# Top-k attention and a low-rank mixer: division by row sums moved to the side of the features, a pair's loads dealt out over four steps

## The chip, the cores and the metric

The kernel runs on one core of a Trainium2 chip. The metric is device time in microseconds; lower is better. All data are 32-bit floats.

## The reference

Attention over 8 batches, 8 heads, 576 positions and 64 features keeps for each query the 32 largest scores, and its output goes through a mixer: a low-rank mix over positions, then a two-layer network over the 512 channels.

```python
scores = scale * np.matmul(q, k.transpose(0, 1, 3, 2))
kth = np.partition(scores, -32, axis=-1)[..., -32:-31]
scores = np.where(scores >= kth, scores, -1e9)
attn = np.exp(scores - np.max(scores, axis=-1, keepdims=True))
attn = attn / (np.sum(attn, axis=-1, keepdims=True) + 1e-09)
x = heads_side_by_side(np.matmul(attn, v))      # (8, 576, 512)
h = x.transpose(0, 2, 1) @ U @ V                # U: 576x32, V: 32x576
u = x + h.transpose(0, 2, 1)
out = u + np.maximum(u @ w_ch1, 0.0) @ w_ch2    # 512 -> 2048 -> 512
```

## The kernel before

Two heads of one batch make a pair, so there are 32 pairs, four to a batch. The 576 positions are four tiles of 128 (t = 0 to 3) and an end of 64, called NT = 4, in which the two heads' ends lie one above the other in the 128 rows.

The order of the work is written out by hand: nothing is reordered by a planner. The main loop runs over steps. In the first four pairs (20 steps, up to ALONE) each tile has its own step; from pair 4 on (NPAIR) a pair has four steps, and the fourth takes tile 3 and the end together. In step n several tiles are in flight:

- `scores` (L332, L364) and `fold` of the tile after this one: PE's products, ACT's copies (L377), POOL's fold of each row's two halves (L428) and, after DVE's maximum (L430), its second half (L431);
- `front`: DVE's search for the 32 largest (L481 to L516), then ACT's and POOL's masking (L542 to L546) and ACT's exponentials, which sum each row into `den` (L435, L556);
- `blocks` turns the exponentials by 32x32 blocks on DVE (L572) and writes them to DRAM (`away`, issued by SP); `back` reads them as PT one step later (issued by ACT, L587);
- `values` of the tile three steps back: PE multiplies PT by V (L646, L649), with the features on the rows of the result, and ACT copies it to XT (L658). For the end (t = NT) positions are on the rows instead (L633), and ACT multiplies by the inverse sums into X (L641);
- `mixed`, once per pair: PE turns XT so that positions lie on the rows (L672), ACT copies it to X (L676), POOL multiplies by the inverse sums (L677). A step later PE multiplies by U (L688), ACT copies that to Tb (L696), PE multiplies by V (L700) and adds X turned back again in the same PSUM tile (L702), and ACT copies the sum to uT (L710), features on the rows.

The two-layer network of a batch (`mlp`: L742 with relu on ACT at L755, L760, turned back for the output at L784) is cut into single matmuls and dealt out by `fill`, eight times a step. Each fill adds a share to an account and issues matmuls until the account is used up:

```python
MLP_WORK = 2 * NF * NC * S / C
SLOTS, LONG, EARLY = 8, 1.4, 0.91
share = MLP_WORK / (NPAIR * SLOTS * (NT - 1 + LONG))
```

A fill also moves `mixed` on by one `yield`. After the last step the rest of the sixth batch's network runs, and then the last batch's, written out as `closing` with seven half-size products in place of eight (L836).

Loads are issued by SP. For pairs after the fifth q and k come in blocks of 32 features, eight DMAs each (L255, L260), and DVE turns them in one instruction (L302); v takes five DMAs (L284 to L288). `loading(g + 1)` issues q in step t = 0 of pair g, and k and v in step t = 1; the turning at L302 stands at the end of step t = 2.

Of the kernel before, what the change touches and what calls it, by code (L numbers as in the profile page):

```python
# [8 lines left out]
F32 = mybir.dt.float32  # L9
# [3 lines left out]
ALU = mybir.AluOpType  # L13
# [13 lines left out]
def kernel(  # L27
# [28 lines left out]
    nc = tc.nc  # L56
    B, H, S, D = q.shape
    P = 128
# [4 lines left out]
    NT, TAIL = 4, 64  # L63
    MAIN = NT * P
    HALF = S // 2
    assert S == MAIN + TAIL and D == 64 and H % 2 == 0 and C == 512 and TOPK % 8 == 0
    NPAIR = H // 2
    NP = B * NPAIR

    CH = NT + 1  # L70
    ALONE = NPAIR * CH
# [4 lines left out]
    BLK = 32  # L76
# [4 lines left out]
    const = ctx.enter_context(tc.tile_pool(name="const", bufs=1))  # L81
# [16 lines left out]
    ident = const.tile([P, P], F32, name="ident")  # L98
# [5 lines left out]
    vds = [const.tile([P, P], F32, name=f"vd{i}") for i in range(NV)]  # L104
    vts = [const.tile([P, 2, D], F32, name=f"vt{i}") for i in range(NV)]

    xs = [const.tile([P, NT + 1, P], F32, name=f"x{i}") for i in range(2)]
    for i in range(NV):
        nc.gpsimd.memset(vds[i], 0.0)
        nc.gpsimd.memset(vts[i], 0.0)  # L110
    for x in xs:
        nc.gpsimd.memset(x[:, NT, :], 0.0)
    W1Q = F // NT
    w1s = [const.tile([P, NC, W1Q], F32, name=f"w1{i}") for i in range(NT)]
    w2 = const.tile([P, NF, C], F32, name="w2")
    U = const.tile([P, NT + 1, R], F32, name="U")

    V = const.tile([NT * R, S], F32, name="V")
    four = const.tile([P, 1], F32, name="four")
    nc.vector.memset(four, -4.0)  # L120

# [8 lines left out]
    def cols(t):  # L130
        return slice(t * P, t * P + rows(t))

    def at(t):
        return slice(OFF[t], OFF[t] + rows(t))

    def half(h):
        return slice(h * D, (h + 1) * D)
# [96 lines left out]

    raw, qkTs, S2s, uTs, XTs, dens = {}, {}, {}, {}, {}, {}
    probs, PTs, folds, fronts_of = {}, {}, {}, {}
    inverted, aways = set(), {}

    def load(g):

# [2 lines left out]
    def loading(g):  # L243

        b, h0 = g // NPAIR, 2 * (g % NPAIR)
        ld = loads.tile([P, 2 * S], F32, tag="ld", name="ld")
        if blocked(g):
            for i, src in enumerate((q, k)):
                if i:
                    yield  # L250
                for a in range(4):
                    ds = src[b, h0 + a // 2, :, a % 2 * BLK : (a % 2 + 1) * BLK]
                    to = ld[a * BLK : (a + 1) * BLK, i * S : (i + 1) * S]
                    lead = TAIL if i and a >= 2 else 0
                    nc.sync.dma_start(  # L255
                        to[:, lead : lead + MAIN].rearrange("i (t m d) -> i t m d", t=NT, d=BLK),
                        ds[0:MAIN].rearrange("(m i t) d -> i t m d", i=BLK, t=NT),
                    )
                    end = 0 if lead else MAIN
                    nc.sync.dma_start(  # L260
                        to[:, end : end + TAIL].rearrange("i (m d) -> i m d", d=BLK),
                        ds[MAIN:S].rearrange("(m i) d -> i m d", i=BLK),
                    )
            raw[g] = ld
        else:
            tiles = []
            ends = ld[:, 2 * MAIN : 2 * S].rearrange("p (h d) -> p h d", h=2)
            for j, src in enumerate((q, k)):
                t = ld[:, j * MAIN : (j + 1) * MAIN].rearrange("p (t h d) -> p t h d", t=NT, h=2)
                for i in range(2):  # L270
                    queue = nc.scalar if g == 0 and i else nc.sync
                    queue.dma_start(
                        t[:, :, i, :],
                        src[b, h0 + i, 0:MAIN, :].rearrange("(p t) d -> p t d", t=NT),
                    )
                tiles.append(t)
            for i, src in enumerate((q, k)):
                nc.sync.dma_start(
                    ends[half(i)], src[b, h0 : h0 + 2, MAIN:S, :].rearrange("h p d -> p h d")
                )  # L280
            raw[g] = tiles, ends
        va, vd, vt = (a[g % NV] for a in (vas, vds, vts))
        for i in range(2):
            nc.sync.dma_start(  # L284
                va[:, i], v[b, h0 + i, 0:MAIN, :].rearrange("(p t) d -> p t d", t=NT)
            )
            nc.sync.dma_start(vd[half(i), half(i)], v[b, h0 + i, MAIN:S, :])
        nc.sync.dma_start(vt[TAIL:P], v[b, h0 : h0 + 2, MAIN:S, :].rearrange("h p d -> p h d"))  # L288
        yield
# [327 lines left out]
    def inverse(g, lo, hi):  # L617
        den = dens[g][:, lo:hi]
        if g == NPAIR - 1:
            nc.vector.tensor_scalar_add(den, den, 1e-9)  # L620
        nc.vector.reciprocal(den, den)

    def values(g, t):

        PT = PTs.pop((g, t))
        va, vd, vt = (a[g % NV] for a in (vas, vds, vts))
        O = ps_t.tile([P, P], F32, tag="tp", name="O")
        if t == NT:
            den, x = dens[g], xs[g % 2]
            if g not in inverted:  # L630
                inverse(g, 2 * NT if g == NPAIR - 1 else 0, 2 * NT + 1)
            for j in range(NT + 1):
                nc.tensor.matmul(  # L633
                    O,
                    lhsT=PT[:, j],
                    rhs=va[:, :, j, :] if j < NT else vt,
                    start=(j == 0),
                    stop=(j == NT),
                )
            for h in range(2):  # L640
                nc.scalar.mul(x[half(h), NT, half(h)], O[half(h), half(h)], den[half(h), 2 * NT :])  # L641
            return
        if shared(g, t):
            PT = PT.rearrange("p c n -> p (c n)")
            PT = PT.rearrange("p (a c j) -> p c a j", a=4, j=BLK)
        nc.tensor.matmul(O, lhsT=vd, rhs=PT[:, 2 * NT], start=True, stop=False)  # L646
        for j in range(NT):
            for h in range(2):
                nc.tensor.matmul(  # L649
                    O[half(h)],  # L650
                    lhsT=va[:, h, j, :],
                    rhs=PT[:, NT * h + j],
                    start=False,
                    stop=(j == NT - 1),
                )
        if t == 0:
            XTs[g] = attn.tile([P, MAIN], F32, tag="XT", name="XT", bufs=1)
        nc.scalar.copy(XTs[g][:, cols(t)], O)  # L658


    def mixed(g, wait, lag=0):
# [4 lines left out]
        if gi == 0:  # L666
            uTs[b] = mlpp.tile([P, NC, S], F32, tag="uT", name="uT")
        XT, den = XTs.pop(g), dens[g]
        X = xs[g % 2]
        tp = ps_t.tile([P, NT, P], F32, tag="tp", name="tp")  # L670
        for t in range(NT):
            nc.tensor.transpose(tp[:, t, :], XT[:, cols(t)], ident)  # L672
        X4 = X[:, 0:NT, :].rearrange("p t (h d) -> p t h d", h=2)
        tp4 = tp.rearrange("p t (h d) -> p t h d", h=2)
        den4 = den[:, 0 : 2 * NT].rearrange("p (t h) -> p t h ()", h=2).to_broadcast([P, NT, 2, D])
        nc.scalar.copy(X4, tp4)  # L676
        nc.gpsimd.tensor_tensor(X4, X4, den4, ALU.mult)  # L677
        if wait is None:
            waiting.append(g)
            while g in waiting:  # L680
# [5 lines left out]
        for t in range(NT + 1):  # L686
# [5 lines left out]
                start=(t < NT),  # L692
                stop=(0 < t),
            )
        Tb = mlpp.tile([P, P], F32, tag="Tb", name="Tb")
        nc.scalar.copy(Tb, pT)  # L696
        yield
        for chunks, (lo, hi) in zip(PARTS, SPAN):
            up = ps_t.tile([P, WIDE], F32, tag="tp", name="up")
            nc.tensor.matmul(up[:, 0 : hi - lo], lhsT=Tb, rhs=V[:, lo:hi], start=True, stop=False)  # L700
            for t in chunks:
                nc.tensor.matmul(  # L702
                    up[:, OFF[t] - lo : OFF[t] - lo + rows(t)],
                    lhsT=X[:, t, :],
                    rhs=ident if t < NT else ident2,
                    is_transpose=True if t < NT else None,
                    start=False,
                    stop=(t == chunks[-1]),
                )
            nc.scalar.copy(uTs[b][:, gi, lo:hi], up[:, 0 : hi - lo])  # L710
            yield
        if gi == NPAIR - 1:
            fillers.append(closing(b) if b == B - 1 else mlp(b))
# [371 lines left out]
    def tiles(n):  # L1085

        return steps[n] if 0 <= n < STEPS else []

    def weighted(m):

        for g, t in reversed(tiles(m)):
            values(g, t)
        if tiles(m)[-1][1] == NT:
            mixing.append(mixed(g, None, 1) if m < STEPS - 1 else mixed(g, 5, 0))
# [19 lines left out]
    for n in range(STEPS + 2):  # L1114
# [11 lines left out]
        if n >= ALONE - 1 and n <= ALONE:  # L1126
# [33 lines left out]
            next(here)  # L1160
            coming = loading(g + 1)
            next(coming)
            next(here)
            fill()
            continue
# [48 lines left out]
        turn()  # L1214
        fill()
        next(last, None)
        next(here, None)
        next_params(1)
        fill()
        if n >= STEPS:  # L1220
            weighted(n - 2)
        elif n - 2 >= ALONE and len(tiles(n - 2)) > 1:
            g2 = steps[n - 2][0][0]
            inverted.add(g2)
            inverse(g2, 0, 2 * NT + 1)
        next(here, None)
        bound = tiles(n + 1)[:1] == [(NPAIR + 1, 0)]
        if not bound:
# [8 lines left out]
            if shared(*tile_):  # L1237
                blocks(*tile_)
        turning = turned(n - 1)
        if n < STEPS and t < 2 and g + 1 < NP:  # L1240
            if t == 0:
                coming = loading(g + 1)
            next(coming)
        next(ready, None)
        if t != 0:
            next_params(1)
# [38 lines left out]
```

## Time and profile before

| what | value |
|---|---|
| median of 3 runs | 1685.39 us (1684.06 to 1687.28) |
| profiled execution: time, span | 1686.28 us, 1684.5 us |
| PE, weight loads, DVE busy | 94%, 72%, 92% of the span |
| ACT, POOL busy | 59%, 56% |
| mean granted clock | 0.969 |
| DMA | 273898 packets, 180.97 MB, 107 GB/s mean |

PE is TensorE's matmul, PEld its weight load, DVE VectorE, ACT ScalarE, POOL GpSimd, SP SyncE; a "q" after a name means its sequencer, which issues DMAs. A 32-bit matmul appears as two records. In a line of a group, "x20 | 14.6, 728" is 20 instructions, 14.6 us of busy time and 728 ns each; what follows is the idle time ahead of them and what ended it. L numbers are lines of the kernel before.

### The profile page before, as it was taken

Reading aid. Unit: us, or ns where it says so; the run is one execution under the profiler, and the core shown is the slowest. Engines: PE = TensorE matmul, PEld = TensorE weight load, DVE = VectorE, ACT = ScalarE, POOL = GpSimd, SP = SyncE. Lnnn points to the kernel's source line nnn. Section 1 sums busy time; section 2 is a strip of 40 time slices with the busy share of each in tenths; the row PEclk is TensorE's granted clock in tenths of the full one; section 3 lists DMA queues with packets and bytes.
Section 4 is the critical chain, followed back from the end, with each engine's and each line's share of the span. In section 5 each row is a group of like instructions: output and inputs, shape, how many; then the busy total and the mean of one; then the engine's idle time right before and its main releaser. Section 6 shows DMA issues by size and latency. Waiting matters only on the chain.

```text
span 1684.5 us, 29512 instructions
## 1 busy us (share of the span) xinstructions
PE 1586.0 (94%) x9498; PEld 1213.4 (72%) x9498; DVE 1543.7 (92%) x4364; ACT 1000.1 (59%) x2475; POOL 939.0 (56%) x741
## 2 busy tenths in 40 slices
PE   4666799999899999999999999999999999999999
PEld 2444466788677887788777887778777887778876
DVE  7999998999999999999999999999999999994452
ACT  4888778665665656565665656565665656554320
POOL 4778668655555555555555555555555455552620
PEclk7788799999999999999999999999999999999999
DMA  3323232254545555554545555554545455533001
GB/s 87 96 75 96 58 91 73 55 133 123 131 110 136 125 131 128 131 129 120 128 117 130 125 130 125 132 125 125 128 115 131 122 134 124 131 105 102 10 1 29
DMA packets 273898, 180.97 MB, mean 107 GB/s; under 512 B 171376, under 2 KB 258256, under 8 KB 273744
## 3 DMA queue, kind: packets, MB, share of 16 engines
q1 hardware_dynamic: 257712, 117.49, 30.2%
q10 hardware_dynamic: 16032, 61.61, 11.7%
q8 instruction: 75, 1.23, 0.3%
q14 instruction: 79, 0.65, 0.1%
HBM read 108.23 MB, written 70.78 MB: 106 GB/s over the span
## 4 chain that ended last, share of the span: by engine, by line
PE 54%; DVE 32%; SPq 4%; DMA 4%; issue 2%; POOL 2%; ACT 1%; DVEq 0%; ACTq 0%; POOLq 0%
PE mm L760 16%; PE mm L742 16%; DVE m L516 10%; DVE upper L511 9%; PE sc L332 4%; PE O L649 4%; DVE first L498 3%; PE mm L836 3%; DVE y L572 3%; DVE upper L483 2%; PE sc L836 2%; PE tp L836 2%; DVE place L511 2%; DMA ld<-in_k_dram 2%; SPq L255 2%
## 5 line engine op out<-in xcount | busy, mean ns | idle before, releaser
L742 PE MATMUL mm<-uT,w 128*128 128x320 f32 (+1 forms) x1792 | 461.1, 410 | 1.9 <-ACT hT L755 1.9
L760 PE MATMUL mm<-hT,w 128*128 128x320 f32 (+1 forms) x1792 | 461.5, 408 | 0.0
L546 POOL TENSOR_TENSOR Ssb<-Ssb,E 128x576 f32<-128x576 f32 x243 | 339.4, 1416 | 210.7 <-ACT E L545 210.4
L742 PEld LDWEIGHTS mm<-uT,w 128*128 128x128 f32 x1792 | 333.7, 191 | 97.5 <-issue 12.0
L760 PEld LDWEIGHTS mm<-hT,w 128*128 128x128 f32 x1792 | 330.5, 190 | 90.3 <-issue 10.2
L516 DVE MAX8 m<-upper 128x8 f32<-128x304 f32 (+1 forms) x780 | 367.4, 512 | 0.7
L511 DVE MATCH_REPLACE8 upper<-m,upper 128x304 f32<-128x304 f32 (+1 forms) x520 | 259.9, 507 | 0.0
L431 POOL TENSOR_TENSOR lower<-lower,upper 128x576 uint32<-128x576 uint32 x108 | 152.3, 1410 | 157.5 <-DVE upper L430 152.6
L428 POOL TENSOR_TENSOR lower<-Ssb 128x576 uint32<-128x576 uint32 x108 | 152.4, 1411 | 144.0 <-ACT Ssb L377 87.0
L435 ACT ACTIVATE Ssb<-Ssb,nmax 128x576 f32<-128x576 f32 x258 | 200.8, 780 | 22.3 <-POOL Ssb L522 10.1
L332 PE MATMUL sc<-qkT 64*128 64x288 f32 (+1 forms) x1056 | 178.8, 460 | 10.8 <-ACT Ssb L386 7.8
L545 ACT ACTIVATE E<-Ssb,least 128x576 f32<-128x576 f32 x243 | 176.2, 768 | 4.2
L483 DVE MAX8 upper<-lower 128x8 f32<-128x288 f32 x432 | 172.2, 440 | 6.9 <-POOL lower L431 6.9
L377 ACT COPY Ssb<-sc 128x576 f32<-128x576 f32 x216 | 127.6, 643 | 69.2 <-PE sc L332 69.1
L572 DVE STREAM_TRANSPOSE y<-Ssb 128x512 f32<-128x512 f32 (+1 forms) x312 | 155.4, 547 | 8.8 <-ACT Ssb L435 8.8
L755 ACT ACTIVATE hT<-mm 128x320 f32<-128x320 f32 (+1 forms) x224 | 92.1, 411 | 112.2 <-PE mm L742 107.4
L649 PE MATMUL O<-PT,va 128*64 128x128 f32 x2048 | 145.1, 286 | 0.0
L332 PEld LDWEIGHTS sc<-qkT 64*128 64x128 f32 (+1 forms) x1056 | 95.7, 197 | 51.2 <-issue 16.4
L649 PEld LDWEIGHTS O<-PT,va 128*64 128x64 f32 x2048 | 113.8, 141 | 16.3 <-issue 1.6
L511 DVE MATCH_REPLACE8 upper<-first,upper 128x304 f32<-128x304 f32 x216 | 97.7, 460 | 0.0
L481 DVE MATCH_REPLACE8 lower<-upper,lower 128x288 f32<-128x288 f32 x216 | 94.1, 444 | 0.0
L430 DVE TENSOR_TENSOR upper<-sc,Ssb 128x576 f32<-128x576 f32 x108 | 80.3, 744 | 12.7 <-ACT Stail L397 12.4
(250 smaller groups left out, 2201.3 us busy)
## 6 DMA issues: line engine op xcount, KB each, us to landing
away<-y SPq DMA_DIRECT2D x416, 144.0 KB, 2.5
PT<-away ACTq DMA_DIRECT2D x104, 576.0 KB, 3.9
raw<-in_moe_w_ch_dram SPq DMA_DIRECT2D x32, 512.0 KB, 3.8
va<-in_v_dram SPq DMA_DIRECT2D x64, 128.0 KB, 2.6
out_dram<-ob SPq DMA_DIRECT2D x59, 128.0 KB, 2.5
ld<-in_q_dram SPq DMA_DIRECT2D x108, 64.0 KB, 3.1
ld<-in_k_dram SPq DMA_DIRECT2D x108, 64.0 KB, 2.6
ld<-in_q_dram SPq DMA_DIRECT2D x108, 8.0 KB, 3.2
```

Of the source, the lines that this page charges most:

```text
L332: nc.tensor.matmul(out, lhsT=qkT[half(h), 0, cols(t)], rhs=qkT[half(h), 1, lo:hi], start=True, stop=True,)
L428: nc.gpsimd.tensor_tensor(bottom, a.bitcast(U32), b.bitcast(U32), ALU.add)
L435: nc.scalar.activation(E, chunk, AF.Exp, bias=nmax, scale=SCALE, accum_out=total)
L483: nc.vector.max(spot, lower)
L511: nc.vector.match_replace(nxt, ms[c], curs[c], NEG)
L516: nc.vector.max(ms[c], curs[c])
L545: nc.scalar.activation(gap, chunk, AF.Relu, bias=least[:, c : c + 1], scale=-WIDEN)
L546: nc.gpsimd.tensor_tensor(chunk, chunk, gap, ALU.subtract)
L572: nc.vector.transpose(y[:, :, i * NT : i * NT + c].rearrange("p r c j -> p c r j"), E2[:, a : a + c * P].rearrange("p (c r j) -> p c r j", ...
L649: nc.tensor.matmul(O[half(h)], lhsT=va[:, h, j, :], rhs=PT[:, NT * h + j], start=False, stop=(j == NT - 1),)
L742: nc.tensor.matmul(ph[:, 0:w], lhsT=first_layer(cc, f), rhs=uT[:, cc, lo:hi], start=(cc == 0), stop=(cc == NC - 1),)
L760: nc.tensor.matmul(po[:, 0:w], lhsT=w2[:, f, c * P : (c + 1) * P], rhs=hTs[f][:, 0:w], start=(f == 0), stop=(f == NF - 1),)
```

## The change

For the 28 pairs from NPAIR on, the division moves. The inverse sums are turned on DVE, written to DRAM in rows (four DMAs from SP), and read back as a tile `sc` that has features on the rows and the inverse sum of each position along them (four DMAs from ACT, broadcast over 64 rows each). POOL multiplies XT by it into uT. PE turns uT (and its end) for the product with U only; L702 is left out, and POOL adds the product with V to uT instead. The end's values are computed with features on the rows, 64 columns at a time. X and Tb have one buffer instead of two. Values of a step run in the order tile 3, end. The loads of a pair start one step sooner and are dealt out: q, half of k, half of k, v.

```diff
@@ -104,18 +104,19 @@
...
-    xs = [const.tile([P, NT + 1, P], F32, name=f"x{i}") for i in range(2)]
+    X = const.tile([P, NT + 1, P], F32, name="x")
...
+    upright = const.tile([P, BLK], F32, name="upright")
+    nc.vector.memset(upright, 0.0)
...
@@ -249,6 +250,8 @@
                 if i:
                     yield
                 for a in range(4):
+                    if i and a == 2:
+                        yield
                     ds = src[b, h0 + a // 2, :, a % 2 * BLK : (a % 2 + 1) * BLK]
                     to = ld[a * BLK : (a + 1) * BLK, i * S : (i + 1) * S]
                     lead = TAIL if i and a >= 2 else 0
@@ -262,6 +265,7 @@
                         ds[MAIN:S].rearrange("(m i) d -> i m d", i=BLK),
                     )
             raw[g] = ld
+            yield
         else:
             tiles = []
             ends = ld[:, 2 * MAIN : 2 * S].rearrange("p (h d) -> p h d", h=2)
@@ -618,7 +622,33 @@
         den = dens[g][:, lo:hi]
         if g == NPAIR - 1:
             nc.vector.tensor_scalar_add(den, den, 1e-9)
-        nc.vector.reciprocal(den, den)
+        if g < NPAIR:
+            nc.vector.reciprocal(den, den)
+            return
+        inverted.add(g)
+        nc.vector.reciprocal(upright[:, 0 : 2 * NT + 1], den)
+        turned_ = small.tile([P, BLK], F32, tag="rows", name="rows", bufs=1)
+        nc.vector.transpose(turned_, upright)
+        rd = dram.tile([2 * NT + 1, P], F32, tag="rd", name="rd")
+        scales[g] = rd
+        for a in range(4):
+            nc.sync.dma_start(
+                rd[:, a * BLK : (a + 1) * BLK], turned_[a * BLK : a * BLK + 2 * NT + 1]
+            )
+
+    def scale(g):
+
+        rd = scales.pop(g)
+        sc = attn.tile([P, S], F32, tag="scale", name="scale", bufs=1)
+        scales[g] = sc
+        for h in range(2):
+            nc.scalar.dma_start(
+                sc[half(h), 0:MAIN].rearrange("p (t n) -> p t n", t=NT),
+                rd[0 : 2 * NT].rearrange("(t h) n -> h t n", h=2)[h : h + 1].to_broadcast([D, NT, P]),
+            )
+            nc.scalar.dma_start(
+                sc[half(h), MAIN:S], rd[2 * NT : 2 * NT + 1, half(h)].to_broadcast([D, TAIL])
+            )
 
     def values(g, t):
 
@@ -626,7 +656,19 @@
         va, vd, vt = (a[g % NV] for a in (vas, vds, vts))
         O = ps_t.tile([P, P], F32, tag="tp", name="O")
         if t == NT:
-            den, x = dens[g], xs[g % 2]
+            if g >= NPAIR:
+                for j in range(NT + 1):
+                    for h in range(2):
+                        nc.tensor.matmul(
+                            O[half(h), 0:TAIL],
+                            lhsT=va[:, h, j, :] if j < NT else vt[:, h, :],
+                            rhs=PT[:, j, half(h)],
+                            start=(j == 0),
+                            stop=(j == NT),
+                        )
+                nc.scalar.copy(XTs[g][:, MAIN:S], O[:, 0:TAIL])
+                return
+            den = dens[g]
             if g not in inverted:
                 inverse(g, 2 * NT if g == NPAIR - 1 else 0, 2 * NT + 1)
             for j in range(NT + 1):
@@ -638,7 +680,7 @@
                     stop=(j == NT),
                 )
             for h in range(2):
-                nc.scalar.mul(x[half(h), NT, half(h)], O[half(h), half(h)], den[half(h), 2 * NT :])
+                nc.scalar.mul(X[half(h), NT, half(h)], O[half(h), half(h)], den[half(h), 2 * NT :])
             return
         if shared(g, t):
             PT = PT.rearrange("p c n -> p (c n)")
@@ -654,7 +696,7 @@
                     stop=(j == NT - 1),
                 )
         if t == 0:
-            XTs[g] = attn.tile([P, MAIN], F32, tag="XT", name="XT", bufs=1)
+            XTs[g] = attn.tile([P, S], F32, tag="XT", name="XT", bufs=1)
         nc.scalar.copy(XTs[g][:, cols(t)], O)
 
 
@@ -666,15 +708,35 @@
         if gi == 0:
             uTs[b] = mlpp.tile([P, NC, S], F32, tag="uT", name="uT")
         XT, den = XTs.pop(g), dens[g]
-        X = xs[g % 2]
+        uT = uTs[b][:, gi]
+        if g >= NPAIR:
+            sc = scales.pop(g)
+            pairs_ = [
+                a[:, 0:MAIN].rearrange("p (b n) -> p b n", b=2) for a in (XT, sc)
+            ]
+            ends = [uT[:, OFF[t] : OFF[t] + 2 * P] for t in (0, 2)]
+            for i, end in enumerate(ends):
+                nc.gpsimd.tensor_tensor(end, pairs_[0][:, i], pairs_[1][:, i], ALU.mult)
+            nc.gpsimd.tensor_tensor(uT[:, at(NT)], XT[:, MAIN:S], sc[:, MAIN:S], ALU.mult)
+            yield
+            yield
         tp = ps_t.tile([P, NT, P], F32, tag="tp", name="tp")
         for t in range(NT):
-            nc.tensor.transpose(tp[:, t, :], XT[:, cols(t)], ident)
-        X4 = X[:, 0:NT, :].rearrange("p t (h d) -> p t h d", h=2)
-        tp4 = tp.rearrange("p t (h d) -> p t h d", h=2)
-        den4 = den[:, 0 : 2 * NT].rearrange("p (t h) -> p t h ()", h=2).to_broadcast([P, NT, 2, D])
-        nc.scalar.copy(X4, tp4)
-        nc.gpsimd.tensor_tensor(X4, X4, den4, ALU.mult)
+            nc.tensor.transpose(
+                tp[:, t, :], XT[:, cols(t)] if g < NPAIR else uT[:, at(t)], ident
+            )
+        X4 = X[:, 0:NT, :]
+        nc.scalar.copy(X4, tp)
+        if g < NPAIR:
+            X4 = X4.rearrange("p t (h d) -> p t h d", h=2)
+            den4 = den[:, 0 : 2 * NT].rearrange("p (t h) -> p t h ()", h=2)
+            nc.gpsimd.tensor_tensor(X4, X4, den4.to_broadcast([P, NT, 2, D]), ALU.mult)
+        else:
+            if g == NPAIR:
+                nc.gpsimd.memset(X[TAIL:P, NT, :], 0.0)
+            tp = ps_t.tile([P, P], F32, tag="tp", name="tp")
+            nc.tensor.transpose(tp[0:TAIL], uT[:, at(NT)], ident)
+            nc.scalar.copy(X[0:TAIL, NT, :], tp[0:TAIL])
         if wait is None:
             waiting.append(g)
             while g in waiting:
@@ -692,13 +754,15 @@
                 start=(t < NT),
                 stop=(0 < t),
             )
-        Tb = mlpp.tile([P, P], F32, tag="Tb", name="Tb")
+        Tb = mlpp.tile([P, P], F32, tag="Tb", name="Tb", bufs=1)
         nc.scalar.copy(Tb, pT)
         yield
         for chunks, (lo, hi) in zip(PARTS, SPAN):
             up = ps_t.tile([P, WIDE], F32, tag="tp", name="up")
-            nc.tensor.matmul(up[:, 0 : hi - lo], lhsT=Tb, rhs=V[:, lo:hi], start=True, stop=False)
-            for t in chunks:
+            nc.tensor.matmul(
+                up[:, 0 : hi - lo], lhsT=Tb, rhs=V[:, lo:hi], start=True, stop=(g >= NPAIR)
+            )
+            for t in chunks if g < NPAIR else ():
                 nc.tensor.matmul(
                     up[:, OFF[t] - lo : OFF[t] - lo + rows(t)],
                     lhsT=X[:, t, :],
@@ -707,7 +771,11 @@
                     start=False,
                     stop=(t == chunks[-1]),
                 )
-            nc.scalar.copy(uTs[b][:, gi, lo:hi], up[:, 0 : hi - lo])
+            if g < NPAIR:
+                nc.scalar.copy(uT[:, lo:hi], up[:, 0 : hi - lo])
+            else:
+                nc.scalar.copy(sc[:, lo:hi], up[:, 0 : hi - lo])
+                nc.gpsimd.tensor_tensor(uT[:, lo:hi], uT[:, lo:hi], sc[:, lo:hi], ALU.add)
             yield
         if gi == NPAIR - 1:
             fillers.append(closing(b) if b == B - 1 else mlp(b))
@@ -1088,7 +1156,7 @@
 
     def weighted(m):
 
-        for g, t in reversed(tiles(m)):
+        for g, t in tiles(m):
             values(g, t)
         if tiles(m)[-1][1] == NT:
             mixing.append(mixed(g, None, 1) if m < STEPS - 1 else mixed(g, 5, 0))
@@ -1159,6 +1227,7 @@
             split(*steps[n + 1][0])
             next(here)
             coming = loading(g + 1)
+            next(coming)
             next(coming)
             next(here)
             fill()
@@ -1214,15 +1283,16 @@
         turn()
         fill()
         next(last, None)
+        if n < STEPS and n - 2 >= ALONE and len(tiles(n - 2)) > 1:
+            scale(steps[n - 2][0][0])
         next(here, None)
         next_params(1)
         fill()
         if n >= STEPS:
+            if n == STEPS:
+                inverse(NP - 1, 0, 2 * NT + 1)
+                scale(NP - 1)
             weighted(n - 2)
-        elif n - 2 >= ALONE and len(tiles(n - 2)) > 1:
-            g2 = steps[n - 2][0][0]
-            inverted.add(g2)
-            inverse(g2, 0, 2 * NT + 1)
         next(here, None)
         bound = tiles(n + 1)[:1] == [(NPAIR + 1, 0)]
         if not bound:
@@ -1237,10 +1307,12 @@
             if shared(*tile_):
                 blocks(*tile_)
         turning = turned(n - 1)
-        if n < STEPS and t < 2 and g + 1 < NP:
-            if t == 0:
-                coming = loading(g + 1)
-            next(coming)
+        if n < STEPS and n - 1 >= ALONE and len(tiles(n - 1)) > 1:
+            inverse(steps[n - 1][0][0], 0, 2 * NT + 1)
+        if n < STEPS:
+            if t == NT - 1:
+                coming = loading(g + 2) if g + 2 < NP else iter(())
+            next(coming, None)
         next(ready, None)
         if t != 0:
             next_params(1)
```

More of the change, by code (lines that the diff above doesn't have):

```diff
@@ L110 @@
         nc.gpsimd.memset(vts[i], 0.0)
-    for x in xs:
-        nc.gpsimd.memset(x[:, NT, :], 0.0)
+    nc.gpsimd.memset(X[:, NT, :], 0.0)
     W1Q = F // NT
@@ L236 @@
     probs, PTs, folds, fronts_of = {}, {}, {}, {}
-    inverted, aways = set(), {}
+    inverted, aways, scales = set(), {}, {}
     def load(g):
```

## The prediction

> **What bounds the kernel now.** I read the page first: PE is busy for 94% of the span and DVE for 92%, so the shares alone don't decide. Next I read the table of windows over the steady part, in 50 us stretches (columns: wall time, then PE, weight load, DVE, ACT and POOL busy, granted clock, DMA share, GB/s):
>
> ```profile
> 850.00:900.00 50.00, 50.00 (x289) 36.17 (x288) 49.52 (x150) 29.56 (x74) 29.10 (x23) 1.00 0.51 130
> 900.00:950.00 50.00, 50.00 (x312) 39.91 (x311) 47.92 (x143) 29.65 (x77) 26.73 (x21) 1.00 0.50 124
> ```
>
> PE fills its stretches, DVE leaves about 1 us per pair of heads free. Then the chain of waits from 840 to 960 us, which is PE from end to end. Here is one step and the start of the next (start, length, what, records):
>
> ```profile
> 890.43 1.11 PE O L633 x10
> 891.55 0.22 PE O L646 x2
> 891.77 1.02 PE O L649 x16
> 892.79 1.18 PE sc L364 x14
> 893.97 1.17 PE sc L332 x8
> 895.14 1.27 PE mm L760 x4
> 896.42 0.44 PE tp L672 x4
> 896.85 4.85 PE mm L760 x18
> ...
> 906.62 0.74 PE up L700 x2
> 907.35 0.39 PE up L702 x4
> 907.74 1.13 PE mm L760 x4
> 908.87 0.43 PE up L700 x2
> 909.31 0.22 PE up L702 x2
> ```
>
> Each piece starts where the one before ends: PE is back to back, and a 320-column record takes 4.85/18 = 0.27 us, which is its full rate. From about 448 to 1493 us no PE record starts late by more than its usual spacing, over 22 pairs of 47.4 us. So a saving on PE counts in full there, a new PE wait counts in full, and a DVE wait counts for nothing until PE has given up about 1 us per pair. Before 448 us (pairs 4 to 6) DVE is full and the pair takes 46.4 us; after 1493 us PE works off what is left and then closes.
>
> **What the Trainium skill says.** "TensorEngine Tiling (Array Packing)", section Key Properties: column tiles run their weight loads and matmuls in parallel, and a change of tiling mode drains the array. The trace agrees: 16 records of L649 (64 columns, 128 moving) take 1.02 us, 0.064 each, where a 128-column record of L633 takes 0.11. "GPSIMD Engine Reference", section 3.1 Elementwise, has POOL at about twice DVE's time for an add; the trace shows POOL's own times, used below. "DMA: Bandwidth & Descriptors", Rules for kernel authors, wants the issuing engine to wait on the semaphore of a DMA whose bytes it reads back through another DMA. No wait of that length is on PE's chain before; the new inverse sums need one, on ACT.
>
> **The change part by part, per changed pair** (28 of them, 22 in the PE-bound stretch).
>
> *PE, removed.* The second turning of X, L702: 0.39 + 0.22 = 0.61 us. *PE, added:* one turning of the 64-row end, priced as one of the four of L672: 0.44/4 = 0.11. *PE, changed:* the tail's values, L633, 10 records of 128x128 in 1.11 us, become 20 records of 64 columns by 64 moving, in the tiling mode of L649. Upper bound: L649's 0.064 each, 1.28 us, that is 0.17 more than now. Lower bound: each moves half the columns, and L649's 1.02 contains a change of mode that the tail right behind it doesn't pay again (estimated 0.15 us): (1.02 - 0.15)/16/2 x 20 = 0.54. I take 0.56, because L649 shows its records running side by side: saved 0.55. Sum on PE: -0.61 + 0.11 - 0.55 = **-1.05 us** (ends -0.33 and -1.07).
>
> *PE, a new wait.* Before, L672 turns XT as soon as ACT has copied it, and PE waits for nobody. Now POOL first multiplies XT by the scales into uT, and PE turns uT two fills later. Is two fills enough? In the order of the code the multiplications stand behind this step's fold on POOL. The timeline gives that queue:
>
> ```profile
> 896.02 1.42 POOL L428 TENSOR_TENSOR lower<-Ssb 128x576 uint32<-128x576 uint32 x1 [1.90 <-issue]
> 897.93 1.04 POOL L677 TENSOR_TENSOR x<-x,den 128x512 f32<-128x512 f32 x1 [0.50 <-ACT x L676]
> 898.93 1.40 POOL L431 TENSOR_TENSOR lower<-lower,upper 128x576 uint32<-128x576 uint32 x1
> ```
>
> L428 ends at 897.44, 2.3 us after the scores end at 895.14, and it hangs on those scores through ACT's copies, so it can't come earlier relative to PE. POOL's price for 128x256 is this group:
>
> ```profile
> L772 POOL TENSOR_TENSOR oT<-oT,uT 128x256 f32<-128x256 f32 x20 | 14.6, 728 | 30.3 <-ACT oT L771 27.3 <-DVE upper L430 3.0
> ```
>
> 128x320 takes 865 ns and 128x576 1411 there, so 2.13 ns per element, and 128x64 about 0.32 us. The three products then end 0.73, 1.46 and 1.78 us after L428, near 898.2, 898.9 and 899.2. PE arrives earlier: a fill carries share = 1.02 units of 512 columns, 1.64 matmuls of 320 columns at 2 x 0.27 us, 0.88 us. Three fills after the scores PE stands at 895.14 + 2.64 = 897.8, could be through five turnings (0.55) at 898.3, but gets the last operand at about 899.2 and ends near 899.3. **A wait of 1.0 us**; with POOL's products a third quicker 0.5, and 1.5 if every turning waits for all three products. Queued behind it are this step's remaining fills and the next step's scores, thus everything.
>
> *ACT.* Two scaled copies of the tail (L641, 2 x 0.3) go, two copies of 64 columns or rows come (0.26 each, as L788): nothing. Added are four issues of broadcast loads: the existing ACT issue, PT<-away, takes 0.33 us, SP's small ones 0.58 to 0.65, so 1.3 to 2.6 us of ACT's queue, in the middle of the step after the pair's last turning on DVE. They also wait for the four writes of the sums: DVE ends those turnings about 3 us after the sums are ready, SP issues four away writes (1.75 us) and then the four small ones (about 1.8), which land 2.5 us later; ACT reaches the loads after its second exp at about the same moment, within 1 us. Behind stand the relus of L755. PE's double buffer forgives a lag of one group of eight records, 8 x 0.27 = 2.15 us for 320 columns and 1.73 for 256, and only half of the pairs are in the first layer then. I take 0.1 us of PE in those, 0.05 over all (0 to 0.6).
>
> *DVE.* One more turning, 128x32: from 271 ns at 128x128 and 685 at 128x512, 0.17 us; the inverse itself is moved, 0.2 us. Covered by the 1 us of slack; without that cover it would cost 0.17 per pair, and does so on the DVE-bound pairs: +0.5 us in all.
>
> *POOL.* L677 (1.04) goes, the three products (1.78) and two adds (0.87 + 0.73) come: +2.3 us on an engine with 20 us of 47 free. L431 comes about 0.4 us later, and DVE's next use of it comes 0.5 to 2.7 us after its end now: hidden, barely.
>
> *SP and the loads.* 21 issues of a pair now stand in two steps, 8 and 13 (0.58 to 0.65 us each for q and k); they will be dealt 8, 4, 4 and 5, with the first eight a step before. The wait they can end is DVE's L302 on ld, 5.2 us in 6 waits (3.3 and 1.1 more put down to issue and va) between 400 and 1500 us, about 0.4 us a pair. That lies in DVE's slack. Nothing gained while PE binds, up to 0.4 a pair where DVE does. The four small writes of the sums fit the freed room.
>
> *One buffer for X and Tb instead of two:* both are read a step before they are written again: nothing.
>
> *The end.* The last pair's sums go through DRAM too, ahead of its turnings on DVE, and SP issues four writes ahead of four away writes: about 2 us on that chain, and two fills later for its mixing. The leftover of the layer before fills PE up to 1570 us while uT is complete at 1563.8, so 4 of some 5 us are hidden. I take +0.5 us (0 to 4).
>
> **Sum.** Stretch: 22 x (-1.05 + 1.0 + 0.05) = 0. DVE-bound pairs: +0.5, less some of their load waits, 0. The end +0.5. That is +0.5 on the profiled execution's own 1686.3 us (span 1684.5 and 1.8 around it), which stands 0.9 above the median of 1685.4. I lay it on the median, rounded down since the end's cost is the least sure: **1685.5 us, no change**. PE loses in one new wait what it gains in work.
>
> **Rivals.**
> *The wait is hidden* (faster). If POOL's products are ready when PE comes, for instance because the first two turnings overlap the second product fully, PE gives up 0.5 to 1.0 us per pair, until DVE's 46.4 us binds with its own short waits: 22 x 0.5 to 0.8, 1668 to 1674.5 us. For it: PE really is the only bound, the removed rows are certain. Against: L428 hangs rigidly on the scores.
> *ACT is held by the sums' way through DRAM* (slower). Place: the four loads ahead of the relus, one step in four. It decides once the writes land over 1 us after ACT's second exp, as ACT's lag then passes 2.15 us; each further half microsecond costs as much on PE: 22 x 0.5 = 11 us, 1696. For it: SP's queue is busy in just that step. Against: the loads dealt out relieve that queue.
> *The change moves loads that nothing waited for:* that part is inside the forecast.
>
> **How the numbers follow.** 0.2% is 3.4 us, about what a measurement of this kernel can tell from no change. No change 0.42, faster 0.33 (the wait half hidden or better), slower 0.25 (ACT held, or all turnings wait for all products). The ends: 22 x -0.55 = -12, 1673; 22 x +0.5 = +11, 1696.
>
> **What would show it.** Right: L702 rows of 128 columns gone, the 20 records at about 0.6 us, and a PE wait of about 1 us on POOL before the turnings of uT, once per pair; the pair still near 47.4 us; L302's waits gone without effect. Wrong: no such wait, and a pair under 47 us; or waits of PE on ACT's relu after the broadcast loads.

## The result and the profile after

| | before | after |
|---|---|---|
| median | 1685.66 us (10 runs) | 1681.22 us (10 runs) |
| profiled execution: time, span | 1686.28, 1684.5 us | 1681.84, 1679.8 us |

The ratio is 0.9974, 95% interval 0.9965 to 0.9982: 4.4 us faster, 0.26%. The forecast was no change (1685.5 us); the time lies inside the stated range, but the change is faster beyond what the measurement leaves open.

The windows of the changed kernel, columns as before (wall time; PE, weight load, DVE, ACT, POOL busy; clock; DMA share; GB/s). From here on an L number is a line of the kernel whose trace is shown:

```profile
850.00:900.00 50.00, 49.19 (x295) 34.66 (x294) 49.85 (x150) 29.03 (x74) 32.01 (x29) 1.00 0.52 131
900.00:950.00 50.00, 49.49 (x317) 38.64 (x316) 48.34 (x146) 29.30 (x77) 28.53 (x24) 1.00 0.55 135
```

PE no longer fills its stretches: 0.8 and 0.5 us are missing from the two. The chain of waits shows where (start, length, what, records):

```profile
895.78 0.77 DVE upper L434
...
896.86 1.46 POOL uT L719 x2
...
898.36 0.44 PE tp L725 x2
898.79 0.14 PE tp L738
898.94 3.23 PE mm L828 x12
...
907.08 0.74 PE up L762 x2
907.82 1.08 PE mm L828 x4
908.90 0.43 PE up L762 x2
909.33 5.92 PE mm L828 x22
```

The chain passes through POOL's products (L719) into PE's turnings of uT (L725); before, POOL was nowhere on it between 840 and 960 us. It comes to POOL by way of DVE's L434, for which POOL's sequencer had just waited on behalf of a later instruction; the engine itself was at its fold (L432) until 896.9, as the timeline below shows. After the product with V (L762) the network's matmuls follow at once; the 0.39 and 0.22 us of L702 are gone. The timeline has the same place engine by engine (start, length, engine, line, operation; idle time before it in brackets):

```profile
891.52 0.63 PE L662 MATMUL O<-PTt,va 128*64 128x64 f32 x16
891.99 0.29 PE L662 MATMUL O<-PTt,vt 128*64 128x64 f32 x4
...
894.55 2.96 PE L828 MATMUL mm<-hT,w 128*128 128x320 f32 x10
895.50 1.41 POOL L432 TENSOR_TENSOR lower<-Ssb 128x576 uint32<-128x576 uint32 x1 [1.35 <-issue]
896.86 1.45 POOL L719 TENSOR_TENSOR uT<-XT,scale 128x256 f32<-128x256 f32 x2
897.67 0.44 PE L725 MATMUL tp<-ident,uT 128*128 128x128 f32 x2 [0.16 <-POOL uT L719]
898.24 0.35 POOL L720 TENSOR_TENSOR uT<-XT,scale 128x64 f32<-128x64 f32 x1
898.36 0.44 PE L725 MATMUL tp<-ident,uT 128*128 128x128 f32 x2 [0.25 <-POOL uT L719]
```

The scores end where L828 starts, at 894.55; POOL's fold holds the products until 896.86, and PE has done its three fills (ten records) before the first product is there. The prices of POOL and the waits on uT between 448 and 1490 us (a group; then who waited, us, times):

```profile
L719 POOL TENSOR_TENSOR uT<-XT,scale 128x256 f32<-128x256 f32 x44 | 31.6, 741 | 0.0
L720 POOL TENSOR_TENSOR uT<-XT,scale 128x64 f32<-128x64 f32 x22 | 7.3, 332 | 0.0
```
```profile
  PEld tp L725: 24.1, 44
  PE tp L725: 6.8, 28
```

In each of the 22 pairs PE's weight load waited twice. To see what the whole change did to PE, I summed the distance from each PE record's start to the next one's over the same 22 pairs of both traces, from 370.0 to 1413.0 us before and from 372.0 to 1412.4 after (us; a wait counts with the record ahead of it). Below this sum is called the account of PE's starts:

```
                          before   after   per pair
X turned back (L702)       13.35    0.00    -0.61
values of the end          25.17   14.98    -0.46
values of the tiles        91.01   88.81    -0.10
turnings of XT or uT       13.66   25.46    +0.54
network, both layers      680.11  691.86    +0.53
all else                  219.68  219.25    -0.02
sum                      1042.98 1040.36    -0.12
```

Work removed is 1.17 us a pair. Added is 1.07: a fifth turning (0.13), a wait for POOL of about 0.87 (0.74 to 0.99 in 21 of the 22 pairs; in the other, PE also waits some 4 us in both kernels), which stands partly with the network's record ahead of it, and 0.07 of longer waits for relus. That is 2.6 us over the 22 pairs; moved two pairs later, the same sum gives 2.9. The other 2 us came at the end: the first record of the closing network (L836, now L904) starts at 1565.7 in place of 1570.3 us, 4.7 earlier, of which 2.6 had gathered by the last pair but one.

### The profile page after: what moved, and what is told of

Read it like the earlier page. It is cut to its first block, busy times and chain, and to the rows that moved or that the text cites. A ratio compares the mean times of both kernels' runs of the same rounds, so it can differ in the third digit from the quotient of the medians.

```text
span 1679.8 us, 30303 instructions
## 1 busy us (share of the span) xinstructions
PE 1571.6 (94%) x9638; PEld 1183.9 (70%) x9638; DVE 1547.1 (92%) x4393; ACT 991.1 (59%) x2475; POOL 1000.2 (60%) x853
## 4 chain that ended last, share of the span: by engine, by line
PE 58%; DVE 25%; POOL 5%; DMA 4%; ACT 3%; issue 2%; SPq 2%; ACTq 0%; DVEq 0%; POOLq 0%
PE mm L828 17%; PE mm L810 16%; DVE m L520 7%; DVE upper L515 7%; PE sc L336 5%; PE O L691 5%; PE mm L904 3%; DVE first L502 2%; DVE y L576 2%; DVE upper L487 2%; PE sc L904 2%; PE tp L904 2%; DMA ld<-in_k_dram 2%; POOL uT L719 2%; PE up L762 1%
## 5 line engine op out<-in xcount | busy, mean ns | idle before, releaser
L828 PE MATMUL mm<-hT,w 128*128 128x320 f32 (+1 forms) x1792 | 462.1, 407 | 0.0
L828 PEld LDWEIGHTS mm<-hT,w 128*128 128x128 f32 x1792 | 332.3, 190 | 93.0 <-issue 10.2
L432 POOL TENSOR_TENSOR lower<-Ssb 128x576 uint32<-128x576 uint32 x108 | 152.6, 1413 | 139.1 <-ACT Ssb L381 52.2
L700 ACT COPY XT<-O 128x128 f32<-128x128 f32 x128 | 33.8, 264 | 111.3 <-PE O L691 103.8
```

What stands on the lines that cost most here:

```text
L828: nc.tensor.matmul(po[:, 0:w], lhsT=w2[:, f, c * P : (c + 1) * P], rhs=hTs[f][:, 0:w], start=(f == 0), stop=(f == NF - 1),)
```

## The experiments

All ratios are to the kernel before, with 95% intervals, from runs on the same chip; its medians there were 1684.7 to 1686.1 us, so times of different runs compare to about 1 us. Sums of waits are from the view of waits between 448 and 1490 us, which counts waits of at least 0.15 us, unless the account is named. The theories: **A**, PE paces the steady part, and the change gains by PE work less one wait on POOL. **B**, the loads gave the gain. Two more came up on the way.

**The loads alone.** The kernel before with the loads dealt out and nothing else.

```diff
+                    if i and a == 2:
+                        yield
...
-        if n < STEPS and t < 2 and g + 1 < NP:
-            if t == 0:
-                coming = loading(g + 1)
-            next(coming)
+        if n < STEPS:
+            if t == NT - 1:
+                coming = loading(g + 2) if g + 2 < NP else iter(())
+            next(coming, None)
```

> The kernel before with nothing but the loads dealt out over four steps (8, 4, 4, 5 issues, the first eight a step earlier). Theory A (PE paces the steady part, the change gained by PE work saved less one PE wait on POOL's products): DVE's waits on ld go, PE's chain does not change, so within 2 us of before, 1684 to 1687 us. Theory B (the gain of 4.4 us came from the loads): 1680 to 1682 us.

Measured: 1685.58 us, ratio 0.9998 (0.9990 to 1.0006). DVE's waits ahead of the turning of ld went from 9.6 us to none, and the time moved to another wait of DVE, ahead of L430 (L433 in this run):

```profile
DVE upper L430 <- ACT Stail L397: 8.1, 15, 0.9
DVE upper L433 <- ACT Stail L400: 18.4, 20, 1.9
```

B falls: a wait removed from an engine that does not pace comes back at its next wait.

**The division without the loads.** The changed kernel with the same diff undone.

> The changed kernel with the loads put back where they were (8 and 13 issues in two steps). Theory A: within 2 us of the changed kernel, 1679 to 1683 us, with DVE's waits on ld back and no PE wait more. Theory B: back to 1685 to 1686 us.

Measured: 1737.5 us, ratio 1.0310 (1.0297 to 1.0323). Both theories missed, by over 50 us: the loads give nothing alone, and the division needs them. The profiled execution is the slowest of the four (1742.0 us). Its timeline at one of the places where PE stood still:

```profile
962.69 0.62 ACTq L642 DMA_DIRECT2D scale<-rd  x1
962.83 0.63 SPq L261 DMA_DIRECT2D ld<-in_q_dram  x1
963.35 0.63 ACTq L646 DMA_DIRECT2D scale<-rd  x1
963.50 0.58 SPq L256 DMA_DIRECT2D ld<-in_q_dram  x1
...
966.69 0.62 ACTq L642 DMA_DIRECT2D scale<-rd  x1
...
967.36 0.63 ACTq L646 DMA_DIRECT2D scale<-rd  x1
...
968.03 0.21 ACT L503 ACTIVATE nmax<-first 128x2 f32<-128x2 f32 x1 [5.50 <-DMA ld<-in_q_dram]
968.14 0.64 ACT L820 ACTIVATE hT<-mm 128x256 f32<-128x256 f32 x2
968.56 1.65 PE L807 MATMUL mm<-uT,w 128*128 128x256 f32 x3 [3.94 <-ACT hT L820]
```

ACT issues two broadcast loads and then stands 2.7 us ahead of the third. What released it is a landing of q, not a write of the sums: in the trace SP's and ACT's transfers take turns at eight completion semaphores, and one that comes round to a semaphore waits for the transfer that used it last. The third load's semaphore had last been used by a load of q that SP issued at 960.78 us; that load's last count came at 966.67, and ACT went on at 966.69. So an unrelated load of SP holds ACT, two relus stand behind it, and PE waits 3.94 us. The waits of PE for relus between 448 and 1490 us show the size (engine, line, waited for: us, times, longest):

```profile
PEld mm L807 <- ACT hT L820: 33.8, 23, 4.5
PE mm L807 <- ACT hT L820: 25.4, 12, 4.1
```

The two rows overlap in part. In the account of PE's starts the same waits are 45 us more than before the change, of 53 us by which the 22 pairs are longer.

**One fill, and three.** The changed kernel with PE's turnings one fill after the products, then three, in place of two; the last pair as it was.

```diff
             yield
-            yield
+            if wait is not None:
+                yield
```
```diff
             yield
             yield
+            for _ in range(1 if wait is None else 0):
+                yield
```

> The changed kernel with PE's turnings of uT one fill after POOL's products instead of two (the last pair kept as it is). Theory A: PE comes one fill, 0.88 us, sooner and waits that much longer in each of some 24 pairs: +19 to +21 us, about 1701 us, and the wait before the turnings goes from about 0.9 to about 1.7 us. If the wait does not set the pace (theory B): within 3 us of 1681.

Measured: 1708.35 us, ratio 1.0135 (1.0120 to 1.0149), 27 us over the changed kernel. The wait sets the pace: by the view of who waited on uT the weight loads waited 42.4 us where the changed kernel has 24.1. The time is above theory A's number, but per pair it is of A's size: the 22 pairs of the account are 20.4 us longer, 0.93 each. The profiled execution is 25.4 us longer in all; 1.8 of the rest lie in the pair ahead of the 22, 1.6 in the two pairs behind them, and 1.7 behind the last scores, where one more such pair is turned; some 0.8 us of that I have not explained.

> The changed kernel with PE's turnings of uT three fills after POOL's products instead of two (the last pair kept). Theory A: the wait of about 0.9 us falls to 0.1 or less, and PE gives up that much per pair until DVE binds (46.4 us a pair in DVE's own work, 47.2 now): 0.6 to 0.85 us times 22 pairs, 13 to 19 us, so 1663 to 1668 us. Theory B: within 3 us of 1681.

Measured: 1681.45 us, ratio 0.9980 (0.9972 to 0.9989), with single runs from 1677.7 to 1689.2. The wait ahead of the turnings went as expected (turnings of uT in the account: 25.5 to 16.0 us), and nothing was gained. PE had a new wait instead, in the view of waits:

```profile
PEld mm L812 <- ACT hT L825: 18.5, 16, 3.0
PE mm L812 <- ACT hT L825: 12.6, 8, 2.6
```

These are the relus again, in an execution that is the slowest of the 22 (1689.2 us), so the sums are large for this kernel. With PE further ahead, ACT's hold at the fourth broadcast load (some 38 us in 21 pairs, against 12 in 8 pairs of the changed kernel) seems to show on PE. That is theory **C**: the trip through DRAM holds ACT, and ACT's relus hold PE. Its rival **D** for the old loads: they are simply too late for DVE.

**The broadcast loads issued by SP.** They stand right behind the four writes, a step earlier; the last pair's stay with ACT.

```diff
-            nc.scalar.dma_start(
+            (nc.scalar if g == NP - 1 else nc.sync).dma_start(
...
-        if n < STEPS and n - 2 >= ALONE and len(tiles(n - 2)) > 1:
-            scale(steps[n - 2][0][0])
...
             inverse(steps[n - 1][0][0], 0, 2 * NT + 1)
+            scale(steps[n - 1][0][0])
```

With the loads where they were:

> The changed kernel with the loads where they were (as the run at 1737.5 us) and the four broadcast loads of the inverse sums issued by SP right behind the four writes, a step earlier, in place of ACT (the last pair's still by ACT). Theory C (the old loads cost 56 us because ACT, in whose queue the broadcast loads stand ahead of the relus, is held until a load of q that SP issued before them has landed): ACT is free, PE's waits on the relu (59 us between 448 and 1490 us) go, and at least half of the 56 us comes back: 1690 to 1705 us; not all, as SP now holds q and k back by some 5 us and DVE's wait on ld stays. Theory D (the old loads are simply too late for DVE's turning, ACT has nothing to do with it): 1737 us or more.

Measured: 1754.28 us, ratio 1.0414 (1.0400 to 1.0428). A miss for C: slower still, as D's number had it. PE's waits for relus did fall, from 59.2 to 37.6 us (the two rows summed), but DVE now stood 63.4 us ahead of its turning of ld (34.4 with ACT issuing): SP, in order, waits for the sums to come round through DRAM and issues q and k behind that. Moving the trip from one queue to the other also chose who is held, so this run does not separate C from D.

With the loads dealt out, two fills:

> The changed kernel with the four broadcast loads issued by SP right behind the writes in place of ACT. Theory C: ACT's wait ahead of the fourth one (12 us in 8 of 22 pairs) and the waits on the relu that follow (2 us on PE more than before the change) go: 1677 to 1681 us. Theory D: no change, 1681.

Measured: 1678.51 us, ratio 0.9960 (0.9947 to 0.9974), inside C's range, though its interval overlaps that of the changed kernel. The trace says the same: in the account, what PE's starts within the first layer come late beyond their usual spacing fell from 6.1 to 3.7 us in 22 pairs.

With the loads dealt out, three fills:

> The same, and PE's turnings three fills after POOL's products. Theory C (with three fills PE's wait on POOL had gone, but PE then waited on relus held up behind the broadcast loads): now both are gone and DVE binds with 46.5 us a pair against 47.2 of the changed kernel: 11 to 15 us less, 1666 to 1671 us. If three fills failed for another reason (DVE's pace alone, PE and DVE waiting for each other in turn): 1677 to 1682 us.

Measured: **1664.60 us, ratio 0.9879 (0.9866 to 0.9893)**, some 16 us below the changed kernel: a version that beats both, and 1.4 us below C's range. Its windows:

```profile
850.00:900.00 50.00, 50.00 (x313) 36.05 (x312) 49.97 (x152) 29.79 (x74) 29.86 (x25) 1.00 0.52 130
900.00:950.00 50.00, 50.00 (x324) 40.58 (x323) 49.97 (x152) 31.47 (x84) 30.18 (x27) 1.00 0.54 138
```

PE and DVE are both full. DVE's waits are 0.6 us, where the changed kernel has 14.4, and a pair takes 46.6 us.

**PE's work alone.** The kernel before without L702 for the later pairs.

```diff
-            for t in chunks:
+            for t in chunks if g < NPAIR else ():
```

> The kernel before without its second turning of X (L702) in the 28 later pairs and nothing else; it leaves out adding X to the mix there. Theory A (PE paces the steady part): 0.61 us in each of 22 to 25 pairs, 13 to 15 us less, 1671 to 1673 us, unless DVE's 46.4 us and its waits on ld take back some: 1671 to 1676. If PE's saved time were lost to other waits: 1680 to 1686.

Measured: 1675.05 us, ratio 0.9943 (0.9930 to 0.9955), 9.7 us less, inside theory A's wider range. By the account 13.4 us of PE work went from the 22 pairs, and 8.9 of time; PE's waits grew by 4.4. DVE's waits fell from 21.4 to 13.8 us, and 11.3 of what was left stood ahead of the turning of ld (9.6 before). So the loads, which did not matter while PE was slower, may be what takes the rest back; no run tried both. A saving on PE comes back, but not in full.

**Without the trip through DRAM.** POOL multiplies by a constant tile.

```diff
-        rd = dram.tile([2 * NT + 1, P], F32, tag="rd", name="rd")
...
-                a[:, 0:MAIN].rearrange("p (b n) -> p b n", b=2) for a in (XT, sc)
+                a[:, 0:MAIN].rearrange("p (b n) -> p b n", b=2) for a in (XT, V)
```

> The changed kernel with the loads where they were, and with the inverse sums not sent through DRAM: neither the four writes nor the four broadcast loads are issued, and POOL multiplies by a constant tile of the same size, so the division is left out. Theory C (the 56 us of the old loads come from the trip through DRAM meeting them in the queues of SP and ACT): they go, 1678 to 1686 us. Theory D (the old loads are too late for this order of work by themselves): 1720 us or more.

Measured: 1679.89 us, ratio 0.9960 (0.9944 to 0.9975). The whole loss of the old loads is gone, so D falls: the loss needs both the trip and the old loads. DVE still waited 14.2 us ahead of its turning of ld here, where it waited 34.4 in the run at 1737.5, and lost nothing by it that the measurement shows: the next run, with the loads dealt out, is 2 us shorter, and the intervals overlap. This is C in its wider form, the trip meeting the loads in the queues of SP and ACT. The trip's own traffic is a rival that this run removed too. It does not look like the main cause, as the transfers slowed little: by the semaphores' counts half of the loads of q landed within 3.3 us before the change and within 3.5 in the run at 1737.5, nine in ten within 4.6 and 5.5.

> The changed kernel, loads dealt out, with the same trip through DRAM left out and the constant tile in its place (no division). My sum gives the trip 0.05 us of PE per pair (measured nearer 0.1) and about 0 to 2 us at the end: 1677 to 1681 us, like the run with SP's broadcast loads (1678.5). If the trip costs more than the sum has it: under 1675.

Measured: 1677.93 us, ratio 0.9952 (0.9940 to 0.9965). With the loads dealt out the trip costs some 3 us in all, about what SP's issuing saves; neither is far outside the noise.

> Turnings three fills after the products, loads dealt out, no trip through DRAM and no inverse nor its turning on DVE in the later pairs (no division). If DVE binds at three fills, as its 0.8 us of idle time in 22 pairs says, the 0.2 + 0.2 us that it loses per pair come off the 1664.6 us: 8 to 10 us over 22 to 25 pairs, 1654 to 1658. If PE binds there: 1662 to 1665.

Measured: 1661.97 us, ratio 0.9856 (0.9842 to 0.9869), only 2.6 us less than with the inverse (3.9 by the ratios, whose intervals overlap). The number is the other one that I had named, PE binding. The inverse and its turning took 8.5 us of DVE's work in 22 pairs; with them gone DVE's waits rose from 0.6 to 4.0 us, and the pair stayed at 46.6 us, with PE at 50.00 of 50 us between 900 and 950. At 46.6 both engines bind, and DVE's work alone is not worth saving there; whether PE's alone is, no run tried.

## Why the prediction was wrong, point by point

- *PE bound.* Right for the kernel before, as the run without L702 shows, and for the changed one, as the run with one fill does. That "no PE record starts late" overlooked one wait of 1.5 us for a relu. That "a saving on PE counts in full there" was too simple: of L702's 0.61 us a pair 0.41 came back.
- *PE removed and changed.* 1.16 forecast, 1.17 measured. In the chain of waits the end's values take 0.58 us (`845.01 0.58 PE O L662 x20`; 0.56 forecast). The 64-column records run side by side, as the Trainium skill has it ("TensorEngine Tiling (Array Packing)", Key Properties), and the trace agrees: 20 of them take half of what 10 full ones took, 1.11 us, and every second one starts less than 13 ns after the one ahead.
- *The new wait.* In the place and for the reason given, but **this step failed by its size: 1.0 forecast, about 0.87 measured**, which is 2.9 us over 22 pairs. The fifth turning took 0.13 for 0.11. The products came as forecast (741 and 332 ns).
- *ACT.* 0.05 forecast, 0.07 measured, but that agreement is luck: the cause was not the one I gave. Ahead of the first of the four loads, which needs the four writes, ACT lost nothing in 22 pairs. It is held at the fourth, by landings of other loads. My rival "ACT is held" had the right queue, relus and consequence.
- *The loads.* "Moves loads that nothing waited for" is right of the kernel before (0.9998) and **wrong of the changed one**, where they keep 56 us away. I priced the parts one by one against the kernel before and never the division against the old loads.
- *The sum.* Stretch: 0 forecast, -2.6 measured: a tenth of a microsecond, 22 times, and most of it the wait. The DVE-bound pairs ahead of it: 0 forecast, 0.2 longer measured.
- *The end.* **The other step that failed, in its sign: +0.5 forecast, -2.0 measured** (0.9 up to the last pair's scores, 1.2 from there to the closing network). I let 1 of the longer chain's 5 us show, though my own numbers had 6 us of cover. It was covered: uT was complete at 1561.7 us, and the closing network starts at 1565.7. And I put at nothing that the last pair's PE work falls too, and there without the wait: no fold stands ahead of its products on POOL, and PE's turnings start at 1551.3, after the last product has ended at 1550.3 (lines below).

```profile
1550.02 0.32 POOL L720 TENSOR_TENSOR uT<-XT,scale 128x64 f32<-128x64 f32 x1
1551.29 0.60 PE L725 MATMUL tp<-ident,uT 128*128 128x128 f32 x4
```

The -2.0 rests on one pair of traces, and no run tried the end by itself. Of the 0.9, 0.6 is a wait for a relu near 1493 us that the trace of before has and that of the changed kernel has not. The trace of the loads alone, with the same work on PE as before, has no such wait either, and against it the end gains 0.9 in all.

Together these are the 4.7 us of the two profiled executions. Apart from the end and the loads, the steps were right in kind; a forecast whose sum is a difference of two terms of 1.1 us, times 22, can't tell 0 from -0.12 a pair, and the range said so, while "no change" as the likeliest case claimed more.

What stays open: how much of the old loads' 56 us is ACT held and how much is loads that come late for DVE, since both went with the trip; how much of the 2 us at the end is the change; and some 0.8 us of the run with one fill.

## What to carry to other kernels

An edit that is worth nothing alone can decide what another is worth: dealing out the loads gave nothing to the kernel before and 56 us to the changed one. So cost a new transfer against the queues as they will be, with every wait that its issue brings, landings of unrelated transfers among them. Where a wait goes and no time comes back, look at the next engine in order (here ACT's relus behind a transfer) before calling it the bound: three fills gave nothing, SP's issuing some 3 us, and both together some 16. And where a producer sits in a fixed place of another engine's queue, count how long it takes in units of the consumer's work; one fill more or less was worth 27 us one way.

## What the runs showed that I had not expected

A transfer issued by ACT waits for transfers that have nothing to do with it, through completion semaphores used in turn. With the old loads ACT stood up to 3.7 us ahead of one issue, for q that SP had issued. In the changed kernel it stood 12 us in 8 of 22 pairs, and there in 5 of the 8 for its own load of PT and in 3 for SP's loads of k. The tiles' values, whose own records did not change, became 0.10 us a pair shorter once the end's values ran behind them in the same tiling mode: from the last record of tile 3's values to the next record's start it is 0.20 us before, where the mode changes, and 0.10 after. The change of mode now follows the end's values (0.15 us from their last record to the scores), so the 0.10 is at least in part a cost that moved to the next group; no run tried it by itself.
